# Clustered attention and two feed-forward blocks on one core: weight loads from ScalarE's queue, output transposes later in SyncE's queue, and 35 instead of 62 feed-forward steps issued during the heads

## The chip, the cores and the metric

One core of one Trainium2 chip. The metric is the device time of one execution in microseconds (us). The kernel before took 812.64 us as the median of 3 runs (808.35 to 814.8).

## The reference, cut to what matters

Shapes: 2 batches, 8 heads, 768 positions, head size 64, 16 clusters; then 1536 tokens of width 512, hidden width 2048.

```
q_assign = argmax(q_n @ c_n.T); k_assign = argmax(k_n @ c_n.T)      # cluster of each q and k
scores   = where(q_assign == k_assign, (q @ k.T) / 8, -1e9)
attn     = exp(scores - max) / (sum + 1e-9);  o = attn @ v          # 16 heads in all
x = o as (1536, 512)
x = softplus(x @ w_in1) @ w_out1
x = leaky_relu(x @ w_in2) @ w_out2      # leak 0.01
```

## The kernel before, in words

**Precision.** Matmuls run on f16 pairs: a value is held as a high and a low part, and a product is three matmuls (high by high, high by low, low by high).

**Order of the work.** The program gives every instruction a priority number, lower being more urgent (`at_pri`). A planner fixes each engine's order before the run: on its own model of time it gives an engine the most urgent instruction that is ready. On the chip each engine then takes its queue strictly in that order. A DMA stands in the queue of the engine that issues it, and if it must wait, all behind it in that queue wait too.

**Heads.** Each of the 16 heads goes through: loads of q and k (L173, L174) and v (L180); split and first transpose (`split`, `t<-n`, L197); cluster scores on TensorE (`as`, L206) and the one-hot rows on VectorE; two transposes (`tq<-nq` L232, `tk<-nk` L233); a first pass of scores for the row maximum (TensorE L244, VectorE L251); a third transpose (`tm<-nq`, L259); scores again (L277, L278), exponentials on ScalarE (L284), the product with v (L300 to L318) and the normalisation (L347 to L353). Work on a head starts two heads ahead. After each odd head two transposes (`xth<-xnh`, `xtl<-xnl`, L359) put two heads' output into the feed-forward's input. They stand at priority h+1-4, with head h's own work around h. All DMAs, these included, stand in SyncE's queue (SP).

**Feed-forward.** A stretch of 384 tokens (two per batch) goes through 16 tiles of `layer_in` (12 matmuls each, L414) and 16 steps of `layer_mid` (12 matmuls each, L427); the second block has `layer_in` and `layer_out` (L446). A tile of `layer_in` goes from PSUM through its activation into `g_h` and `g_l`. For batch 0 that is `act_ln_exp`: VectorE L392, ScalarE exp L393, ScalarE ln L394, VectorE L395, ScalarE L396, GpSimd L397, where L395 is the last to read the PSUM tile. For batch 1 it is `act_softplus`: ScalarE L382 and L383 read PSUM, VectorE L384 forms the low part. Exp and ln stand in one table of ScalarE; softplus needs an ACT_TABLE_LOAD. From head 8 on, steps of batch 0 are issued between the heads: `FF_RATE` of them for each of 47 slots, so 62 of 64. Step n has priority 8 + n/4. A step issued there takes its PSUM from a ring of two banks (`pm`). One issued behind the last head takes it from a pool of six (`pm2`), which holds the banks that the heads give back.

**Weights.** Each of four weight matrices comes in 16 pieces of 512 KB (`w_piece`): a load into one of two `st` buffers (L134), three VectorE operations that turn 64-bit floats into 32-bit ones (L142, L145, L148; the last one frees `st`), the high part on ScalarE (L152) and the low part on VectorE (L153). The first 32 pieces come during the heads; the second 32 have their place only when the heads' SBUF is given back.

Of the kernel before, what the change touches and what calls it, by code (L numbers as in the profile page):

```python
# [37 lines left out]
AHEAD = 2  # L38
LEAD_SPLIT, LEAD_ASSIGN, LEAD_MAX, LEAD_M, LEAD_LOAD, LEAD_NORM = 2.5, 2, 4, 2.5, 2, 4

FF_PRI, FF_STEP, FF_RATE = 8, 0.25, 1.333

W_FREE, W_FROM, W_TO, W_PER = 4, 8, 10, 5
W_PRI = ((0, 0.5), (17, 0.3))
# [7 lines left out]
def attn_moe_kernel(  # L52
# [12 lines left out]
    nc = tc.nc  # L65
    V, S, G, PE = nc.vector, nc.scalar, nc.gpsimd, nc.tensor
    B, H, SEQ, D = q.shape
    NCL = cen.shape[1]
    DM, DFF = w_in1.shape
    C = SEQ // 128  # L70
# [21 lines left out]
    def atile(shape, dt, tag, h):  # L92
        late, early = BUFS[tag]
        n = turn[tag] = turn.get(tag, -1) + 1
        if h < H and early and n % (late + early) >= late:
            return ep.tile(shape, dt, tag=tag, name=tag, bufs=early)
        return at.tile(shape, dt, tag=tag, name=tag, bufs=late)

    w_inh = const.tile([128, KDM, DFF], F16, name="w_inh")
    w_inl = const.tile([128, KDM, DFF], F16, name="w_inl")  # L100
    w_outh = const.tile([128, KFF, DM], F16, name="w_outh")
    w_outl = const.tile([128, KFF, DM], F16, name="w_outl")
    xt_h = [const.tile([128, KDM, SEQ], F16, name=f"xth{b}") for b in range(B)]
    xt_l = [const.tile([128, KDM, SEQ], F16, name=f"xtl{b}") for b in range(B)]
# [26 lines left out]

    def w_piece(dsth, dstl, src):
        st = wst.tile([128, 512, 2], I32, tag="st", name="st")
        nc.sync.dma_start(out=st, in_=src.rearrange("p (n t) -> p n t", t=2))  # L134

        def conv(bank=False):
            lo, hi = st[:, :, 0], st[:, :, 1]
            if bank:
                c = pm.tile([128, 512], I32, tag="m0", name="wcp")
            else:  # L140
                c = wst.tile([128, 512], I32, tag="wc", name="wc")
            V.tensor_scalar(  # L142
                out=c, in0=hi, scalar1=3, scalar2=0x3FFFFFFF, op0=ALU.logical_shift_left, op1=ALU.bitwise_and
            )
            V.scalar_tensor_tensor(  # L145
                out=c, in0=hi, scalar=-0x40000000, in1=c, op0=ALU.bitwise_and, op1=ALU.bitwise_or
            )
            V.scalar_tensor_tensor(  # L148
                out=c, in0=lo, scalar=29, in1=c, op0=ALU.logical_shift_right, op1=ALU.bitwise_or
            )  # L150
            cf = c.bitcast(F32)
            S.activation(out=dsth, in_=cf, func=AF.Copy, scale=WS)  # L152
            V.scalar_tensor_tensor(out=dstl, in0=cf, scalar=WS, in1=dsth, op0=ALU.mult, op1=ALU.subtract)  # L153

        return conv
# [8 lines left out]
    def out_pieces(w, wh, wl):  # L164
        wi = w.bitcast(I32)
        for kk in range(KFF):
            yield wh[:, kk, :], wl[:, kk, :], wi[kk * 128:(kk + 1) * 128, :]
# [170 lines left out]
    def emit_norm(h):  # L338
        b, hh = divmod(h, H)
        if hh % 2 == 0:  # L340
            xn_t[h // 2] = [atile([128, C, 128], F16, f"xn{n}", h) for n in "hl"]
        xh, xl = xn_t[h // 2]
        xps = x_t.pop(h)
        xv = xps[:, 0:C * XW].rearrange("p (c d) -> p c d", d=XW)
        dp = xps[:, C * XW:C * XW + C].unsqueeze(2)
        dd = atile([128, C, 1], F32, "dd", h)
        V.tensor_scalar(out=dp, in0=xv[:, :, D:XW], scalar1=1e-9, scalar2=1.0 / XS, op0=ALU.add, op1=ALU.mult)  # L347
        V.reciprocal(out=dd, in_=dp)
        y = atile([128, C, D], F32, "y", h)
        V.tensor_tensor(out=y, in0=xv[:, :, 0:D], in1=dd.to_broadcast([128, C, D]), op=ALU.mult)  # L350
        cs = slice((hh % 2) * D, (hh % 2) * D + D)
        S.copy(out=xh[:, :, cs], in_=y)
        G.tensor_tensor(out=xl[:, :, cs], in0=y, in1=xh[:, :, cs], op=ALU.subtract)  # L353
        for d_ in (tp1, tp2, tpq):
            d_.pop(h)
        if hh % 2 == 1:
            xn_t.pop(h // 2)
            for src, dst in ((xh, xt_h[b]), (xl, xt_l[b])):
                nc.sync.dma_start_transpose(  # L359
                    out=dst[:, hh // 2, :].rearrange("p (c r) -> p c r", c=C), in_=src.rearrange("p c d -> p (c d)")  # L360
                )


    pmx = [pm]
# [9 lines left out]
    def mps_next():  # L374
        if pmx[0] is pm:
            turn["m"] = 1 - turn.get("m", 0)
            return pm.tile([128, 512], F32, tag=f"m{turn['m']}", name="m")
        return pmx[0].tile([128, 512], F32, tag="m", name="m")
# [23 lines left out]
    def layer_in(b, t0, act, wh, wl):  # L402
        xh, xl = xt_h[b], xt_l[b]
        ts = slice(t0, t0 + TB)
        for m in range(KFF):
            hp = mps_next()[:, 0:TB]
            ms = slice(m * 128, (m + 1) * 128)
            ops = []
            for kk in range(KDM):
                ops += [(wh[:, kk, ms], xh[:, kk, ts]), (wh[:, kk, ms], xl[:, kk, ts])]  # L410
            for kk in range(KDM):
                ops += [(wl[:, kk, ms], xh[:, kk, ts])]
            for i, (w_, x_) in enumerate(ops):
                PE.matmul(out=hp, lhsT=w_, rhs=x_, start=(i == 0), stop=(i == len(ops) - 1))  # L414
            act(m, hp)
            yield

    def layer_mid(b, t0):
        xh, xl = xt_h[b], xt_l[b]
        ts = slice(t0, t0 + TB)  # L420
        for m in range(KDM):
            yp = mps_next()[:, 0:TB]
            ms = slice(m * 128, (m + 1) * 128)
            n = 0
            for kk in range(KFF):
                for w_, g_ in ((w_outh, late["h"]), (w_outh, late["l"]), (w_outl, late["h"])):
                    PE.matmul(out=yp, lhsT=w_[:, kk, ms], rhs=g_[:, kk, :], start=(n == 0), stop=(n == 3 * KFF - 1))  # L427
                    n += 1
                if kk % 4 == 3:
                    if kk == KFF - 1:  # L430
                        S.activation(out=xh[:, m, ts], in_=yp, func=AF.Copy, scale=1.0 / WS)
                        V.scalar_tensor_tensor(
                            out=xl[:, m, ts], in0=yp, scalar=1.0 / WS, in1=xh[:, m, ts], op0=ALU.mult, op1=ALU.subtract
                        )
                    yield
# [19 lines left out]
    def pri(x):  # L455
        return int(100000 + 10000 * x)

    @contextmanager
    def at_pri(x):
        old = tc.cur_priority  # L460
        tc.cur_priority = pri(x)
        yield
        tc.cur_priority = old
# [8 lines left out]
    with at_pri(-9):  # L472
# [6 lines left out]
            out=ss[:, 1:2], in0=ss[:, 0:1], scalar1=ss[:, 2:3], scalar2=ss[:, 1:2], op0=ALU.mult, op1=ALU.add  # L479
# [35 lines left out]
    def w_step():  # L515
        w0, wr = W_PRI[cnt["w"] >= 34]
        with at_pri(w0 + wr * (cnt["w"] % 34)):
            if convs:
                n = cnt["w"] - 1
                g = -1 if n < W_FREE else int(W_FROM + (W_TO - W_FROM) * (n - W_FREE) / (32 - W_FREE))  # L520
                g = min(g, max(mark, default=-1), 15)
                bank = n < KDM * DFF // 512
                if g >= 0:
                    with tc.issue_after(mark[g].ins):
                        convs.pop(0)(bank)
                else:
                    convs.pop(0)(bank)
            if wq:
                convs.append(w_piece(*wq.pop(0)))
        cnt["w"] += 1  # L530
# [7 lines left out]
    def moe1():  # L538
        wq.extend(out_pieces(w_out1, w_outh, w_outl))
        for b in range(B):  # L540
            for t0 in range(0, SEQ, TB):
                for _ in layer_in(b, t0, act_softplus if b else act_ln_exp, w_inh, w_inl):
                    w_step()
                    yield
                while (b, t0) == (0, 0) and (wq or convs):
                    w_step()
                for _ in layer_mid(b, t0):
                    w_step()
                    yield

    def moe2():
        for b in range(B):
            for t0 in range(0, SEQ, TB):
# [5 lines left out]
                yield from layer_out(b, t0, w_out2h, w_out2l)  # L559

    ff = m_steps(moe1())

    def chain(h):
# [22 lines left out]
    st = {"credit": 0.0}  # L586
# [72 lines left out]
```

## Time and profile before

| | |
|---|---|
| median of 3 runs | 812.64 us |
| profiled execution, device time | 808.4 us |
| its span in the trace | 806.6 us |
| TensorE busy | 736.2 us (91%) |
| VectorE / ScalarE / GpSimd busy | 408.4 / 328.7 / 175.3 us |
| mean granted TensorE clock | 0.968 |

The trace is of one execution. PE is TensorE, DVE VectorE, ACT ScalarE, POOL GpSimd, SP SyncE's queue of DMAs. L134 is line 134 of the kernel. In a tile's name "out<-in" buffer numbers are left out.

### The profile page before, as it was taken

The numbers are of one execution on the slowest core, as the hardware profiler recorded it, in microseconds if no ns is written. First come the engines' busy times: TensorE is split into PE (matmuls) and PEld (weight loads), VectorE is DVE, ScalarE is ACT, GpSimd is POOL, SyncE is SP. The second block draws the span as 40 slices with busy tenths as digits, with TensorE's granted clock in tenths as the row PEclk, the third lists the DMA queues.
The fourth block names the chain that finished last, engine by engine and source line by source line (L and its number), as shares of the span: only waits on it lengthen the run. The fifth ranks groups of instructions, "written<-read, shape, count | busy, mean of one in ns | idle before, by whom it ended". The sixth has DMA issues, their size and how long they took to land.

```text
span 806.6 us, 13925 instructions
## 1 busy us (share of the span) xinstructions
PE 736.2 (91%) x5664; PEld 454.1 (56%) x5664; DVE 408.4 (51%) x835; ACT 328.7 (41%) x755; POOL 175.3 (22%) x168
## 2 busy tenths in 40 slices
PE   2489989899899888998689999999999999999998
PEld 1167756576657556775355656666645645644643
DVE  4886767778899977237988931301200200200210
ACT  5266655656566533354535512403402411411410
POOL 5156646534344423331310000000000000000000
PEclk9998978979989999999999999999999999999999
DMA  8977445745757465103445400000000000000000
GB/s 197 207 184 136 96 105 129 166 115 137 168 145 164 124 142 113 23 9 116 132 137 176 158 27 1 1 1 1 1 14 27 1 14 26 1 14 27 1 14 26
DMA packets 104880, 66.01 MB, mean 82 GB/s; under 512 B 90992, under 2 KB 95088, under 8 KB 104816
## 3 DMA queue, kind: packets, MB, share of 16 engines
q1 hardware_dynamic: 104816, 65.13, 33.0%
q8 instruction: 44, 0.72, 0.4%
q14 instruction: 20, 0.16, 0.1%
HBM read 43.02 MB, written 3.15 MB: 57 GB/s over the span
## 4 chain that ended last, share of the span: by engine, by line
PE 62%; DMA 16%; DVE 14%; ACT 4%; issue 2%; SPq 1%; POOL 1%; DVEq 0%; ACTq 0%; POOLq 0%
PE m L414 22%; PE m L446 15%; PE m L427 9%; DMA st<-in_moe_w_out_dram 3%; PE x L300 3%; DMA st<-in_moe_w_in_dram 3%; DMA tm<-nq 3%; DMA t<-n 3%; PE s L278 2%; DVE wc L148 2%; PE s L244 2%; DVE wc L145 2%; PE s L277 2%; DVE mm L251 2%; DVE wc L142 2%
## 5 line engine op out<-in xcount | busy, mean ns | idle before, releaser
L384 DVE TENSOR_TENSOR g_l<-mr,g_h 128x384 f16<-128x384 f32 x96 | 53.4, 557 | 205.4 <-ACT mr L383 205.4
L251 DVE TENSOR_REDUCE mm<-s 128x1 f32<-128x384 f32 x192 | 103.0, 551 | 39.0 <-PE s L244 37.5
L286 POOL TENSOR_TENSOR pl<-p 128x768 f16<-128x768 f32 x56 | 83.2, 1490 | 101.6 <-ACT p L284 100.1
L414 PE MATMUL m<-xth,w_inh 128*128 128x384 f16 x256 | 84.9, 333 | 11.9 <-DVE mr L395 11.9
L284 ACT ACTIVATE p<-s 128x384 f32<-128x384 f32 x144 | 67.4, 489 | 54.2 <-PE s L278 49.6
L427 PE MATMUL m<-g_h,w_outh 128*128 128x384 f16 x256 | 84.0, 329 | 1.6 <-DVE mr L395 1.6
L427 PE MATMUL m<-g_l,w_outh 128*128 128x384 f16 x256 | 84.2, 329 | 1.2 <-DVE g_l L384 1.1
L414 PE MATMUL m<-xtl,w_inh 128*128 128x384 f16 x256 | 84.8, 332 | 0.0
L427 PE MATMUL m<-g_h,w_outl 128*128 128x384 f16 x256 | 83.9, 328 | 0.5 <-DVE w_outl L153 0.4
L414 PE MATMUL m<-xth,w_in2h 128*128 128x384 f16 x256 | 83.3, 326 | 0.0
L414 PE MATMUL m<-xtl,w_in2h 128*128 128x384 f16 x256 | 83.3, 326 | 0.0
L382 ACT ACTIVATE g_h<-m 128x384 f16<-128x384 f32 x96 | 46.7, 491 | 86.4 <-PE m L414 86.4
L244 PE MATMUL s<-tk,tq 80*128 80x384 f16 x192 | 67.1, 365 | 15.1 <-DVE mm L251 9.2
L414 PEld LDWEIGHTS <-w_inh 128*128 128x128 f16 x512 | 50.5, 100 | 46.2 <-issue 16.5
L446 PE MATMUL m<-w_out2h,g_h 128*128 128x512 f16 x192 | 72.8, 379 | 0.0
L446 PE MATMUL m<-w_out2l,g_h 128*128 128x512 f16 x192 | 72.8, 379 | 0.0
L446 PE MATMUL m<-w_out2h,g_l 128*128 128x512 f16 x192 | 72.8, 379 | 0.0
L427 PEld LDWEIGHTS <-w_outh 128*128 128x128 f16 x512 | 50.2, 99 | 34.6 <-issue 3.2
L414 PEld LDWEIGHTS <-w_in2h 128*128 128x128 f16 x512 | 50.1, 98 | 33.4
L446 PEld LDWEIGHTS <-g_h 128*128 128x128 f16 x384 | 37.6, 98 | 44.9
L278 PE MATMUL s<-tm,tk 81*128 81x384 f16 x160 | 55.4, 359 | 8.1 <-DMA tm<-nq 7.9
L277 PE MATMUL s<-t 128*128 128x384 f16 x160 | 56.1, 352 | 4.6 <-ACT p L284 4.2
(108 smaller groups left out, 1303.2 us busy)
## 6 DMA issues: line engine op xcount, KB each, us to landing
st<-in_moe_w_in_dram SPq DMA_DIRECT2D x32, 512.0 KB, 4.1
st<-in_moe_w_out_dram SPq DMA_DIRECT2D x32, 512.0 KB, 3.6
qk<-in_q_dram SPq DMA_DIRECT2D x16, 192.0 KB, 3.2
qk<-in_k_dram SPq DMA_DIRECT2D x16, 192.0 KB, 3.1
v<-in_v_dram SPq DMA_DIRECT2D x16, 192.0 KB, 3.5
out_dram<-ob SPq DMA_DIRECT2D x12, 256.0 KB, 2.0
t<-n SPq DMA_TRANSPOSE x16, 4.0
tq<-nq SPq DMA_TRANSPOSE x16, 4.2
```

Of the source, the lines that this page charges most:

```text
L244: PE.matmul(out=o, lhsT=t[0:KS1, c, :], rhs=tk[0:KS1, 3 * j:3 * j + 3, :], start=True, stop=True,)
L251: V.reduce_max(out=mms[h % 2][:, c, j:j + 1], in_=bank[:, 0:3 * 128], axis=AX)
L277: PE.matmul(out=o, lhsT=t1[:, kt, 1, :], rhs=t1[:, 3 * j:3 * j + 3, 0, :], start=True, stop=False)
L278: PE.matmul(out=o, lhsT=t2[0:KS2, kt, :], rhs=tqh[0:KS2, 3 * j:3 * j + 3, :], start=False, stop=True)
L284: S.activation(out=p[:, j, :], in_=sp, func=AF.Exp, scale=scale)
L286: G.tensor_tensor(out=pl, in0=p, in1=pb, op=ALU.subtract)
L300: PE.matmul(out=xps[:, c * XW:(c + 1) * XW], lhsT=pf[:, c * 128:(c + 1) * 128], rhs=v32s[h % V_BUFS][:, kt, :], start=(kt == 0 and c == 0) ...
L382: S.activation(out=late["h"][:, m, :], in_=hp, func=func, scale=scale, alpha=alpha)
L384: V.tensor_tensor(out=late["l"][:, m, :], in0=r, in1=late["h"][:, m, :], op=ALU.subtract)
L414: PE.matmul(out=hp, lhsT=w_, rhs=x_, start=(i == 0), stop=(i == len(ops) - 1))
L427: PE.matmul(out=yp, lhsT=w_[:, kk, ms], rhs=g_[:, kk, :], start=(n == 0), stop=(n == 3 * KFF - 1))
L446: PE.matmul(out=op, lhsT=g_[:, kk, rs], rhs=w_[:, kk, :], start=(n == 0), stop=(n == 3 * KFF - 1))
```

## The change

Three edits. The weight loads (L134) are issued by ScalarE instead of SyncE. The two output transposes (L359) get priority h+1 instead of h+1-4, except for the last pair of each batch, which keeps its place. `FF_RATE` falls from 1.333 to 0.75, so that 35 of the 64 steps of batch 0 are issued during the heads and 29 behind them (before: 62 and 2). The second stretch of batch 0 takes `act_softplus` in place of `act_ln_exp`.

```
-FF_PRI, FF_STEP, FF_RATE = 8, 0.25, 1.333
+FF_PRI, FF_STEP, FF_RATE = 8, 0.25, 0.75
...
-        nc.sync.dma_start(out=st, in_=src.rearrange("p (n t) -> p n t", t=2))
+        S.dma_start(out=st, in_=src.rearrange("p (n t) -> p n t", t=2))
...
-            for src, dst in ((xh, xt_h[b]), (xl, xt_l[b])):
-                nc.sync.dma_start_transpose(
-                    out=dst[:, hh // 2, :].rearrange("p (c r) -> p c r", c=C), in_=src.rearrange("p c d -> p (c d)")
-                )
+            with at_pri(h + 1 if hh < H - 1 else h + 1 - LEAD_NORM):
+                for src, dst in ((xh, xt_h[b]), (xl, xt_l[b])):
+                    nc.sync.dma_start_transpose(
+                        out=dst[:, hh // 2, :].rearrange("p (c r) -> p c r", c=C), in_=src.rearrange("p c d -> p (c d)")
+                    )
...
-                for _ in layer_in(b, t0, act_softplus if b else act_ln_exp, w_inh, w_inl):
+                for _ in layer_in(b, t0, act_softplus if b or t0 else act_ln_exp, w_inh, w_inl):
```

## Rows read from the trace of the kernel before

**Rows 1.** The page: the span, and TensorE's busy tenths in 40 equal slices.
```profile
span 806.6 us, 13925 instructions
...
PE   2489989899899888998689999999999999999998
```
**Rows 2.** One window: start:end, length, busy us (instructions) by engine, clock, DMA.
```profile
380.00:400.00 20.00, 11.29 (x65) 6.16 (x64) 18.17 (x31) 10.68 (x21) 5.35 (x5) 1.00 0.43 136
```
**Rows 3.** The chain that ended last: start us, us, what.
```profile
23.57 8.48 DMA t<-n
...
153.31 5.62 DMA t<-n
...
345.27 1.95 PE m L414 x12
...
467.51 23.89 PE m L427 x146
491.40 31.20 PE m L414 x192
```
**Rows 4.** Waits from 345 to 420 us: who waited for whom, total us, times, longest.
```profile
PE m L414 <- DVE mr L395: 10.7, 7, 2.5
...
PE m L427 <- DVE mr L395: 1.6, 1, 1.6
```
**Rows 5.** Groups by line: names, shapes, count | busy us, mean ns | idle before, releasers.
```profile
L427 PE MATMUL m<-g_l,w_outh 128*128 128x384 f16 x256 | 84.2, 329 | 1.2 <-DVE g_l L384 1.1
...
L277 PE MATMUL s<-t 128*128 128x384 f16 x160 | 56.1, 352 | 4.6 <-ACT p L284 4.2 <-DVE pl L282 0.2
...
L384 DVE TENSOR_TENSOR g_l<-mr,g_h 128x384 f16<-128x384 f32 x96 | 53.4, 557 | 205.4 <-ACT mr L383 205.4
...
L382 ACT ACTIVATE g_h<-m 128x384 f16<-128x384 f32 x96 | 46.7, 491 | 86.4 <-PE m L414 86.4
...
L382 ACT ACT_TABLE_LOAD x2 | 2.6, 1283 | 0.0
```
**Rows 6.** Timelines of TensorE, ScalarE and VectorE around the last head's end.
```profile
361.08 0.33 PE L414 MATMUL m<-xth,w_inh 128*128 128x384 f16 x1
...
354.34 0.87 ACT L284 ACTIVATE p<-s 128x384 f32<-128x384 f32 x2 [0.30 <-PE s L278]
...
359.88 0.55 DVE L350 TENSOR_TENSOR y<-x,dd 128x384 f32<-128x384 f32 x1
```
**Rows 7.** ScalarE's timeline at the first softplus.
```profile
436.82 1.28 ACT L382 ACT_TABLE_LOAD   x1
438.11 0.49 ACT L382 ACTIVATE g_h<-m 128x384 f16<-128x384 f32 x1
```
**Rows 8.** Waits of SyncE's queue from 0 to 345 us, columns as in rows 4.
```profile
SPq L134 <- DVE wc L148: 34.6, 11, 9.0
...
SPq L134 <- DVE wcp L148: 11.4, 5, 5.2
```
**Rows 9.** Timeline of SyncE's queue, at two places: start us, us, engine, line.
```profile
22.82 0.64 SPq L134 DMA_DIRECT2D st<-in_moe_w_in_dram  x1
...
133.46 1.22 SPq L359 DMA_TRANSPOSE xth<-xnh  x1
...
137.92 1.46 SPq L233 DMA_TRANSPOSE tk<-nk  x1
```
**Rows 10.** TensorE's timeline where it waited for two of these transposes.
```profile
141.41 0.49 PE L244 MATMUL s<-tk,tq 80*128 80x384 f16 x2 [1.18 <-DMA tk<-nk]
...
158.97 0.38 PE L206 MATMUL as<-ct,t 128*128 128x16 f16 x9 [2.63 <-DMA t<-n]
```
**Rows 11.** The heads' 300 us and one early window, columns as in rows 2.
```profile
40.00:340.00 300.00, 273.51 (x2899) 195.42 (x2899) 233.18 (x486) 166.89 (x405) 139.51 (x117) 0.91 0.57 131
...
4.00:8.00 4.00, 0.00 (x0) 0.00 (x0) 3.83 (x14) 3.36 (x9) 3.54 (x4) 1.00 0.96 265
```
**Rows 12.** The page's DMA issues: out<-in, KB each, median us to landing.
```profile
t<-n SPq DMA_TRANSPOSE x16, 4.0
```

## The prediction

> **What bounds it now.** I read the slices first, then windows, then the chain of waits, then who waited. In the slices TensorE (PE) is nearly full except in the first two slices and around the twentieth [rows 1]. The window of that one, 380 to 400 us, has PE busy for 11.29 of 20 us and VectorE for 18.17 [rows 2]. The chain ends in whole stages of PE without a gap: from 467.51 us on nothing stands between the stages, and 16 tiles of layer_in take 31.20 us, 1.95 us a tile [rows 3]. So the end is set by PE's work plus PE's idle time ahead of 467 us, and the question for each edit is which idle it removes or adds.
>
> The largest idle after the heads is one kind: PE waits for L395, the last operation of the exp-and-ln softplus that frees a PSUM tile: 10.7 us in 7 waits and 1.6 us once more [rows 4]. One further gap, 1.1 us, is a wait for L384 [rows 5]. Together 13.4 us. The reader is to see why: an exp-and-ln tile crosses engines four times before its PSUM is free, two of them on VectorE, and VectorE is at that time full of weight conversions [rows 2].
>
> **Edit 1, the activation of the second stretch and the later steps.** Although 62 steps are issued during the heads, the second stretch's first tile runs at 345.27 us, when the heads are nearly over [rows 3]. Sixteen tiles change from exp-and-ln to softplus. PSUM is then free after two ScalarE passes of about 491 ns, with one VectorE operation of 557 ns behind them that PE does not wait for directly [rows 5]. The same softplus beside the same conversions ran later in this trace, and its only PE wait was the 1.1 us one [rows 5]. So I remove all 13.4 us and put 2.2 back, for two such stretches instead of one. Bounds on what stays: 0, and 6 us if ScalarE, which now also issues the loads, falls behind on half of the tiles.
>
> The price is the pool. Steps beyond 35 take their banks from the heads, so they wait for the last head's normalisation, which read its bank until 360.43 us (359.88 + 0.55). In the run before, two tiles of this kind had been worked by 361.08, when the next one starts [rows 6]. Now they come after 360.43: two tiles are 3.9 us, less the 0.65 us between 360.43 and 361.08, so **+3.3 us**.
>
> The three tiles that keep the old ring run beside the last head's exponentials (the last at 354.34 [rows 6]), and softplus needs a table switch of 1.28 us [rows 5, 7]. Each return to exp needs another. On the last head's path I count one switch there and one back, 2.6 us, against one tile of 1.95 us that no longer stands between that head's matmuls: **+0.6 us**. Bounds: -2 us (no switch before the last exp) and +5.7 us (three there, three back, 7.7 - 1.95). In this trace the next activation starts at 438.11, right where the load ends [rows 7]. The Trainium skill (ScalarE: Activation LUTs, What ACT_TABLE_LOAD costs) gives the same 1283 ns but adds a drain, about 2.66 us in all for each switch; the trace shows no drain behind the load, and with it the two switches would cost 2.7 us more and the sum end at -7.0.
>
> **Edit 2, weight loads on ScalarE.** For SyncE it removes 64 issues, one of which took 0.64 us [rows 9], and 46.0 us of waiting for L148 in 16 waits during the heads [rows 8]. What stood behind these was mostly not due yet, so I do not credit them as such. One place counts: loads share a queue with transposes, and the t<-n transpose at 153.31 took 5.62 us and PE waited 2.63 us for it; the median is 4.0 [rows 3, 10, 12]. I credit that 1.6 us.
>
> For ScalarE it adds 32 issues during the heads. At 0.45 us (between nothing, if issue hides behind a running activation, and 0.64) they are 14.4 us; ScalarE is busy 166.89 of 300 us there, so they fit [rows 11]. PE's waits for exponentials were 4.2 us [rows 5]; scaled by 14.4/166.89 that is **+0.4 us**. The waits are the greater risk. L152 of the same piece already stands in ScalarE's queue waiting for L148, and the load two pieces on becomes ready at the same moment, so I take no added wait; the upper bound is the 46.0 us. Queued behind a blocked load would be the exponentials (L284), with PE waiting, and the splits of the head two ahead. The other 32 loads come after the heads. From 467.51 on 86 us of the first block (23.89 + 31.20 and a layer_mid of the same 31.20) still stand ahead of the first matmul that needs these weights [rows 3]; that covers them, and what they could hold up is softplus, which is in the 6 us above.
>
> At the start SyncE's queue is full of more urgent work, and the second load comes at 22.82 us [rows 9]. On ScalarE, idle while q and k land, they can go at 2 us. That costs the first heads bandwidth (DMA share is 0.96 at 4 to 8 us, 265 GB/s [rows 11]) and spares the t<-n that took 8.48 us against 4.0 [rows 3, 12]. Ends: +8 us (four more loads ahead of 32 us, 2.1 MB at 265 GB/s) and -4.5 us. I take 0, since the same bytes move either way.
>
> **Edit 3, output transposes later.** Each of six pairs stands further back in SyncE's queue; the two that close a batch stay. At 133.46 the queue stood until head 5's output was there, and loads, tq and tk went out behind it, tk at 137.92; PE then waited 1.18 us for that tk [rows 9, 10]. **-1.2 us**. Bounds: 0, and -8 us if each of the three pairs of batch 0 cost as much and more. Their outputs are not read before the stretch begins, so lateness costs nothing while two buffers hold.
>
> **The sum.** -13.4 + 2.2 + 3.3 + 0.6 - 1.6 + 0.4 - 1.2 = -9.7 us against the profiled execution's 808.4: 798.7. That execution lies 4.2 us under the median of 812.64, so on the scale of the medians **802.9 us**.
>
> **Rivals.**
> - *A: ScalarE stands still behind loads (slower).* The planner places a load where its model says that L148 is done; on the chip VectorE lags, which is what SyncE's waits for it show [rows 8]. If half of the 46.0 us falls on exponentials that PE needs, the sum is -9.7 - 0.4 + 23 = +12.9: 825.5. It decides once more than about 10 of the 46 us reach PE. Against it: ScalarE has 133 us of slack in the heads [rows 11].
> - *B: the start is bound by DMA, and another queue gives no bandwidth.* Loads move ahead of the heads' own data; half of the +8 us stays, and the transposes gain nothing (+1.6): -9.7 + 4 + 1.6 = -4.1: 808.5. For it: the 0.96 share. Against: what comes early is gone later. The Trainium skill (DMA: Bandwidth & Descriptors, Issuing engines are not separate DMA queues) says that DMAs from any engine run on the same 16 DMA engines and interleave; the share in the early window agrees with a shared limit, and the page speaks for this rival.
> - *C: exp and softplus alternate in the last head.* Six switches, +5.7 instead of +0.6, and the pool opens that much later: -4.6: 808.
> - *D: SyncE's relief is large.* -8 instead of -1.2 for edit 3: -16.5: 796.
> - *E: the planner's order hardly changes what SyncE does, and softplus queues behind loads.* Edits 2 and 3 give nothing and 6 us of idle stay: -9.7 + 2.8 + 3.8 = -3.1: 809.5.
>
> **How the numbers follow.** Forecast 0.42, A 0.15, B 0.16, C 0.10, D 0.07, E 0.10. The time is the forecast's. From no change a measurement of this kernel can tell about 1%, 8.1 us: under 804.5 is faster, over 820.8 slower. The forecast lies 1.6 us inside faster, so of its 0.42 I give 0.37 to faster and 0.05 to the same; D is faster; of the 0.36 of B, C and E, 0.30 lie within, 0.03 in faster and 0.03 in slower (B's whole +8 us with part of A's waits); A is slower for 0.13 and within for 0.02. Faster 0.47, same 0.37, slower 0.16. The range runs from 793 (D with no idle left) to 820; the forecast's own is 798 to 808.
>
> **What would show it.** Right: no PE wait for L395 after the heads and a layer_in of 1.95 us a tile once the banks are free; mid steps about 10 us earlier than 467.51 for the last gap; one or two more ACT_TABLE_LOADs than two at L382; a tk without a wait behind L359. Wrong: weight loads in ScalarE's timeline with idle time ahead of exponentials; the first cluster scores or the first tm later than before; L350 of the last head well after 359.88; or PE idle between the last head's products and the first pm2 tile by more than 3 us.

## The result and the profile after

The changed kernel took 823.49 us as the median of 4 runs (821.12 to 828.97), the kernel before 813.29 us beside it (808.35 to 814.8): a ratio of 1.0119, interval 1.0072 to 1.0166. It is slower, where 802.9 us was forecast, and above the range's 820. Run again beside other kernels it took 819.02 us (10 runs), ratio 1.0057 [1.0018, 1.0095]: slower again, though inside the range. The ratios, here and below, use only executions in the faster of the chip's two states and are not the quotients of the medians. The profiled execution of the changed kernel, 828.97 us with a span of 827.1, is the slowest of the first four, and that of the kernel before, 808.4 us, stands at the lower end of its own. So the two traces differ by 20.5 us where the medians differ by 10.2.

The page after, where [rows 1] stood: span, busy time of TensorE, its busy tenths and its clock in 40 slices.
```profile
span 827.1 us, 13824 instructions
...
PE 749.8 (91%) x5664; PEld 459.9 (56%) x5664; DVE 394.8 (48%) x819; ACT 324.7 (39%) x743; POOL 161.7 (20%) x152
...
PE   0398988788988899998998989999999999999998
...
PEclk9998888679998998997999999999999999999999
```
The hole in the twentieth slice is gone, as forecast. The first two slices fell from 2 and 4 to 0 and 3. PE has as many matmuls as before (5664) but is busy for 13.6 us more (736.2 before): it ran more of them at a lower clock. The other 6.9 of the 20.5 us are idle time.

Two windows, columns as in [rows 2, 11]: the one of the old hole, and the heads.
```profile
380.00:400.00 20.00, 18.84 (x104) 10.76 (x104) 9.93 (x20) 8.87 (x18) 0.91 (x1) 0.83 0.27 73
...
40.00:340.00 300.00, 267.23 (x2711) 185.69 (x2710) 227.95 (x481) 161.00 (x389) 135.03 (x113) 0.87 0.58 126
```
From 380 to 400 us PE is busy 18.84 us instead of 11.29, but at a clock of 0.83. In the heads the clock fell from 0.91 to 0.87. ScalarE, which now issues the loads, is no fuller than before, 161.00 us against 166.89; the issuing of a DMA is not counted in this.

The groups that answer to [rows 4, 5], columns as there.
```profile
L415 PE MATMUL m<-xth,w_inh 128*128 128x384 f16 x256 | 87.3, 342 | 5.4 <-DVE xtl L433 2.1 <-DVE mr L396 1.3 <-DVE y L350 1.2
...
L428 PE MATMUL m<-g_l,w_outh 128*128 128x384 f16 x256 | 84.6, 331 | 3.4 <-DVE g_l L385 3.4
...
L385 DVE TENSOR_TENSOR g_l<-mr,g_h 128x384 f16<-128x384 f32 x112 | 62.4, 557 | 220.6 <-ACT mr L384 220.6
```
Lines are one higher than before from L360 on. PE's waits for the exp-and-ln tile (L395, now L396) are down from the 12.3 us of [rows 4] to 1.3, and g_l rose from 1.1 to 3.4: of the 13.4 us forecast to go, 8.7 went. PE's idle time behind the last head fell from 13.5 to 6.9 us, by 6.6, where the terms of edit 1 that stand there (-13.4 + 2.2 + 3.3) gave 7.9. So the tail did about what it should. The rest of the trace is where it was lost.

The start. Row maxima of the first two heads (L256), columns: operation, min/median/max ns, first and last start us. After, a second profile of the same changed kernel (e9_after below), then before.
```profile
L256 DVE TENSOR_REDUCE nq<-mm x2: 173/178/184, 43.1 to 55.5; 128x6 f16<-128x18 f32 x2
```
```profile
L256 DVE TENSOR_REDUCE nq<-mm x2: 174/178/183, 38.8 to 50.5; 128x6 f16<-128x18 f32 x2
```
```profile
L256 DVE TENSOR_REDUCE nq<-mm x2: 177/178/178, 35.1 to 51.0; 128x6 f16<-128x18 f32 x2
```
The first head is 8.0 us later in the first profile and 3.7 in the second, and in the second the next head has already made it up (50.5 against 51.0). Up to 40 us PE had done 8.71 and 12.12 us of work, against 13.21 before: 4.5 and 1.1 us less. Why the first head is late, is in three timelines of the changed kernel: ScalarE's queue, SyncE's queue, TensorE.
```profile
0.77 0.87 ACTq L134 DMA_DIRECT2D st<-in_moe_w_in_dram  x2
...
7.50 0.33 ACTq L134 DMA_DIRECT2D st<-in_moe_w_in_dram  x1
...
13.49 0.34 ACTq L134 DMA_DIRECT2D st<-in_moe_w_in_dram  x1
...
17.46 0.33 ACTq L134 DMA_DIRECT2D st<-in_moe_w_in_dram  x1
...
21.77 0.33 ACTq L134 DMA_DIRECT2D st<-in_moe_w_in_dram  x1
```
```profile
15.76 3.90 SPq L197 DMA_TRANSPOSE t<-n  x1
```
```profile
28.52 0.81 PE L206 MATMUL as<-ct,t 128*128 128x16 f16 x24 [7.19 <-DMA t<-n]
```
Six loads are out by 22 us, where the second one stood at 22.82 before [rows 9]. The t<-n transpose issued at 15.76 landed at 28.48, with the loads of 13.49 and 17.46 among what was in flight beside it, and PE waited 7.19 us for it. The chain and the page, where [rows 3, 12] stood, show the same later on:
```profile
32.52 5.33 DMA t<-n
...
486.66 25.20 PE m L428 x146
511.86 31.20 PE m L415 x192
```
```profile
t<-n SPq DMA_TRANSPOSE x16, 5.4
```
The median t<-n takes 5.4 us, against 4.0. The last gap ends at 486.66, against 467.51 before.

ScalarE's timeline around the last head, where [rows 6, 7] stood:
```profile
365.81 1.28 ACT L383 ACT_TABLE_LOAD   x1
367.11 0.49 ACT L383 ACTIVATE g_h<-m 128x384 f16<-128x384 f32 x1
...
369.06 1.28 ACT L284 ACT_TABLE_LOAD   x1
...
371.24 1.28 ACT L383 ACT_TABLE_LOAD   x1
...
373.43 1.28 ACT L284 ACT_TABLE_LOAD   x1
...
386.08 1.28 ACT L383 ACT_TABLE_LOAD   x1 [3.61 <-PE m L415]
```
Five table loads stand where none stood. The activation follows its load within 20 ns (365.81 + 1.28, then 367.11).

### The profile page after: what moved, and what is told of

The parts are those of the page before. It is cut to its first block, busy times and chain, and to the rows that moved or that the text cites. A ratio compares the mean times of both kernels' runs of the same rounds, so it can differ in the third digit from the quotient of the medians.

```text
span 827.1 us, 13824 instructions
## 1 busy us (share of the span) xinstructions
PE 749.8 (91%) x5664; PEld 459.9 (56%) x5664; DVE 394.8 (48%) x819; ACT 324.7 (39%) x743; POOL 161.7 (20%) x152
## 3 DMA queue, kind: packets, MB, share of 16 engines
q10 hardware_dynamic: 9216, 33.56, 13.7%
## 4 chain that ended last, share of the span: by engine, by line
PE 63%; DMA 18%; DVE 14%; ACT 2%; issue 2%; SPq 0%; POOL 0%; ACTq 0%; DVEq 0%; POOLq 0%
PE m L415 23%; PE m L447 15%; PE m L428 9%; DMA st<-in_moe_w_in_dram 4%; DMA st<-in_moe_w_out_dram 4%; DMA t<-n 3%; PE x L300 3%; DMA tm<-nq 3%; PE s L278 3%; PE s L244 3%; DVE wc L145 2%; DVE wc L148 2%; DVE mm L251 2%; DMA tk<-nk 2%; PE s L277 2%
## 5 line engine op out<-in xcount | busy, mean ns | idle before, releaser
L385 DVE TENSOR_TENSOR g_l<-mr,g_h 128x384 f16<-128x384 f32 x112 | 62.4, 557 | 220.6 <-ACT mr L384 220.6
L415 PE MATMUL m<-xth,w_inh 128*128 128x384 f16 x256 | 87.3, 342 | 5.4 <-DVE xtl L433 2.1
L383 ACT ACTIVATE g_h<-m 128x384 f16<-128x384 f32 x112 | 54.6, 487 | 87.4 <-PE m L415 87.3
L415 PE MATMUL m<-xtl,w_inh 128*128 128x384 f16 x256 | 87.1, 341 | 0.3 <-DMA xtl<-xnl 0.3
L244 PE MATMUL s<-tk,tq 80*128 80x384 f16 x192 | 69.0, 380 | 13.4 <-DVE mm L251 8.3
L415 PEld LDWEIGHTS <-w_inh 128*128 128x128 f16 x512 | 51.8, 102 | 41.3 <-issue 10.9
L278 PE MATMUL s<-tm,tk 81*128 81x384 f16 x160 | 57.8, 374 | 10.9 <-DMA tm<-nq 10.9
```

The costliest lines, as they stand in the source:

```text
L244: PE.matmul(out=o, lhsT=t[0:KS1, c, :], rhs=tk[0:KS1, 3 * j:3 * j + 3, :], start=True, stop=True,)
L278: PE.matmul(out=o, lhsT=t2[0:KS2, kt, :], rhs=tqh[0:KS2, 3 * j:3 * j + 3, :], start=False, stop=True)
L383: S.activation(out=late["h"][:, m, :], in_=hp, func=func, scale=scale, alpha=alpha)
L385: V.tensor_tensor(out=late["l"][:, m, :], in0=r, in1=late["h"][:, m, :], op=ALU.subtract)
```

## The experiments

Each kernel was timed beside the kernel before on the same chip, in three rounds. Edit 1 is the feed-forward edit, edit 2 the loads, edit 3 the output transposes. "First row max" is the start of L256 of head 0; "last head" is the start of its last L350, whose end is 0.55 us later; both are of one profiled execution.

| kernel | median us | ratio to before, 95% | first row max / last head / span |
|---|---|---|---|
| before | 812 to 816 | 1 | 35.1 / 359.9 / 806.6 |
| after | 823.49 | 1.0119 [1.0072, 1.0166] | 43.1 / 381.4 / 827.1 |
| e9_after (the same again) | 819.02 | 1.0057 [1.0018, 1.0095] | 38.8 / 365.6 / 810.6 |
| e1_loads (edit 2 alone) | 819.27 | 1.0062 [1.0029, 1.0095] | 39.1 / 378.2 / 820.9 |
| e2_ff (edit 1 alone) | 813.09 | 1.0008 [0.997, 1.0046] | 34.1 / 363.6 / 807.4 |
| e3_tr (edit 3 alone) | 807.43 | 0.9919 [0.9883, 0.9955] | 33.6 / 358.2 / 809.0 |
| e4_ff_tr (edits 1 and 3) | 807.13 | 0.9947 [0.9909, 0.9985] | 33.9 / 356.4 / 801.5 |
| e5_first6 | 812.42 | 0.9990 [0.9958, 1.0022] | 34.4 / 367.9 / 810.5 |
| e7_first6act | 811.75 | 0.9993 [0.9961, 1.0026] | 41.3 / 370.0 / 814.9 |
| e6_w2act | 812.82 | 1.0006 [0.9967, 1.0044] | 33.9 / 363.1 / 805.9 |
| e8_mix | 803.84 | 0.9896 [0.984, 0.9952] | 33.8 / 355.6 / 802.2 |
| e10_hold | 823.83 | 1.0162 [1.0097, 1.0228] | 36.9 / 377.9 / 822.0 |
| e11_sliver | 812.24 | 0.9987 [0.9958, 1.0017] | 34.9 / 357.8 / 808.3 |
| e12_mix85 | 801.76 | 0.9878 [0.9832, 0.9924] | 34.3 / 363.1 / 803.1 |
| e13_lite | 803.92 | 0.9778 [0.9681, 0.9874] | 34.5 / 365.9 / 803.6 |
| e14_litesp | 787.18 | 0.9639 [0.9582, 0.9695] | 33.1 / 348.4 / 785.9 |
| e15_replan_sp | 812.80 | 1.0013 [0.997, 1.0056] | 34.1 / 364.4 / 811.5 |
| e16_replan_act | 812.86 | 1.0029 [0.9983, 1.0075] | 38.3 / 367.4 / 810.6 |
| e17_replan2_sp | 814.01 | 1.0021 [0.998, 1.0063] | 37.2 / 360.8 / 805.8 |
| e18_replan2_act | 816.26 | 1.0061 [1.0018, 1.0105] | 39.1 / 371.6 / 815.0 |

### One edit at a time

The diffs are those of the change, each applied alone to the kernel before; the fourth has edits 1 and 3.

e1_loads, only edit 2: 

> Only the weight loads go to ScalarE; the rest is the kernel before. Theory S (the loads cost the time: six go out within 22 us and take DMA bandwidth from the first heads, later ones run beside the transposes and slow them): +12 to +18 us over before, first row maximum (L256) at about 43 us instead of 35, t<-n over 5 us in the median. Theory F (the feed-forward edit costs the time: table switches and the wait for the banks at the last head): within 3 us of before. Theory T (the later output transposes hold up SyncE's queue): within 3 us of before.

e2_ff, only edit 1: 

> Only the feed-forward edit: FF_RATE 0.75 and softplus for the second stretch; loads and output transposes as before. Theory S: 4 to 9 us faster than before, since the 13.4 us of waits for the old activation go and only some come back as table switches. Theory F: 5 us or more slower than before, with at least four table loads at the last head. Theory T: as theory S. First row maximum at 35 us in all of them.

e3_tr, only edit 3: 

> Only the later output transposes. Theory S and theory F: within 3 us of before. Theory T: 5 us or more slower, with heads 6 to 8 late by that much while the first row maximum stays at 35 us.

e4_ff_tr, edits 1 and 3: 

> The changed kernel with all weight loads back on SyncE. Theory S: 12 to 20 us faster than the changed kernel, so 803 to 812, first row maximum at 35 us. Theory F: still 5 us or more over before. Theory T: still 5 us or more over before, lost between heads 5 and 8.

Edit 2 alone makes the kernel slower, edit 1 alone changes nothing that can be measured, edit 3 alone is faster. With the loads back on SyncE the other two edits gave 0.9947. Theory S held for e4_ff_tr (803 to 812), but missed the size of each single edit: 12 to 18 us for edit 2 was 5 by the ratio (6.9 by the medians), 4 to 9 us gained by edit 1 was nothing, and edit 3, expected within 3 us, was 6.6 faster. Nor do the single effects add up: by the ratios they are +5.0, +0.7 and -6.6 us, -0.9 together, and the kernel with all three is 4.6 and 9.7 us slower than the kernel before. The first row maximum is at 34 us in each kernel with loads on SyncE and at 39 to 43 us with them on ScalarE.

Why edit 1 gives nothing: the table loads of e2_ff, and windows from 345 to 370 us (length, PE busy, clock, DMA share, GB/s) of e2_ff, then of before.
```profile
L382 ACT ACT_TABLE_LOAD x5 | 6.4, 1283 | 3.7 <-PE m L414 3.6
...
L284 ACT ACT_TABLE_LOAD x3 | 3.8, 1283 | 0.1
```
```profile
345.00:370.00 25.00, 21.01 (x181) 0.87 0.09 17
```
```profile
345.00:370.00 25.00, 25.00 (x201) 1.00 0.09 17
```
Seven of these loads stand between 348 and 369 us, on both sides of the last head's exponentials. PE, full before, is idle for 4.0 of 25 us there and the clock falls to 0.87. PE's idle time after the last head did fall, from 13.5 to 5.9 us. That head ended 3.7 us later and PE's busy time rose by 7.3 us (736.2 to 743.5), so the span gained nothing (806.6 and 807.4). Up to 350 us e2_ff has TensorE's order of before. So the planner's order in the heads plays no part here; and the lower clock from 40 to 160 us (0.86 against 0.89), which makes up part of the 7.3 us, is a difference between two executions of the same order.

### Which loads cost the time

e5_first6, the first six loads on SyncE and the rest on ScalarE; e7_first6act, the reverse; e6_w2act, the first 32 on SyncE:
```
-        S.dma_start(out=st, in_=src.rearrange("p (n t) -> p n t", t=2))
+        turn["w"] = turn.get("w", -1) + 1
+        (nc.sync if turn["w"] < 6 else S).dma_start(out=st, in_=src.rearrange("p (n t) -> p n t", t=2))
```


> The changed kernel with the first six weight loads back on SyncE, the other 58 on ScalarE. Theory S-start (edit 2 costs through the six loads in the first 22 us alone): all of the 14 us by which the changed kernel and the one with all loads on SyncE differ comes back, 807 to 811, first row maximum at 34 to 35 us. Theory S-middle (it costs in heads 5 to 8, where loads on a queue of their own slow the heads' transfers): 815 to 820, first row maximum at 35 us but row maximum 8 still 10 us late against 156. Half each: about 814.

> The complement: the first six loads on ScalarE, the other 58 on SyncE, edits 1 and 3 as changed. Theory S-start: 819 to 824, as the changed kernel, first row maximum at 40 to 43 us. Theory S-middle: 807 to 812, the late start made up by head 3 (in the run with edit 2 alone row maximum 3 was on time again). Half each: about 815.

> The changed kernel with the first 32 loads (those during the heads) on SyncE and the second 32 on ScalarE. Both theories of edit 2 put its cost into the heads: 805 to 810, the same as with all loads on SyncE (807). If ScalarE is held up behind the late loads (my prediction's rival A, after the heads): 812 or more, with PE idle over 10 us after the last head.

With the first six back on SyncE the start is restored (34.4), with only these on ScalarE it is not (e7_first6act, a line lower):
```profile
L257 DVE TENSOR_REDUCE nq<-mm x1: 171/171/171, 41.3 to 41.3; 128x6 f16<-128x18 f32 x1
```
So the early loads are what moves the start. But all three totals lie within 0.2% of before and 0.4 to 0.6% above e4_ff_tr, also where the early loads are on SyncE. The total isn't explained by the start alone: the total of e7_first6act, late at the start, came out where the theory of a start made up later put it (807 to 812). The parts do not add up either. e9_after, the changed kernel again, was expected at 813 to 816 if the two partial moves' costs added, and took 819.02. The 812.82 us of e6_w2act fit the total of rival A's theory, but PE's idle time after the last head is 4.4 us there and not over 10: the late loads did not hold up ScalarE.

e10_hold keeps all loads on ScalarE and ties the first six behind work of head 0 to 2:
```
+        n = turn["w"] = turn.get("w", -1) + 1
+        if n < 6:
+            with tc.issue_after(held[("el", "m", "m")[n // 2], max(0, n // 2 - 1)].ins):
+                S.dma_start(out=st, in_=src.rearrange("p (n t) -> p n t", t=2))
```


> All loads stay on ScalarE, but the first six are queued behind head work there: two behind head 0's one-hot rows (about 15 us), two behind its row maximum (about 36 us), two behind head 1's. If the early cost is the bytes that go ahead of the heads' own loads: first row maximum back at 34 to 37 us and 4 to 8 us faster than the changed kernel beside it. If it is the second queue as such: first row maximum at 39 us or later and no gain.

It did not recover; it is the slowest of all. The first row maximum came back (36.9) and then the second head lost more. Two queues, ScalarE, VectorE and TensorE of e10_hold:
```profile
37.11 0.35 ACTq L138 DMA_DIRECT2D st<-in_moe_w_in_dram  x1
37.50 0.54 ACTq L138 DMA_DIRECT2D st<-in_moe_w_in_dram  x1
38.08 2.13 SPq L265 DMA_TRANSPOSE tm<-nq  x1
...
46.95 0.69 DVE L148 TENSOR_SCALAR wcp<-st 128x512 int32<-128x512 int32 x1 [6.16 <-DMA st<-in_moe_w_in_dram]
...
48.97 0.51 ACT L199 CAST nq<-qk 128x384 f16<-128x384 f32 x1 [11.55 <-DMA tm<-nq]
```
```profile
48.41 0.48 PE L250 MATMUL s<-tk,tq 80*128 80x384 f16 x1 [7.10 <-DVE mm L257]
```
With two loads and the heads' own transfers in flight beside it, the tm<-nq issued at 38.08 landed at 48.89, after 10.8 us (the median of its kind is 2.9 in before), and a conversion at the head of VectorE's queue waited 6.16 us for the late load, with the row maxima that PE needed behind it. So it isn't how early the loads are, but what they land beside and what waits for them.

e11_sliver lets ScalarE issue 16 of the 512 columns of each piece and SyncE the rest:
```
-        nc.sync.dma_start(out=st, in_=src.rearrange("p (n t) -> p n t", t=2))
+        sr = src.rearrange("p (n t) -> p n t", t=2)
+        S.dma_start(out=st[:, 0:16], in_=sr[:, 0:16])
+        nc.sync.dma_start(out=st[:, 16:512], in_=sr[:, 16:512])
```


> Edits 1 and 3 with every load split: ScalarE issues the first 16 of 512 columns of each piece, SyncE the other 496. ScalarE's queue so carries the 64 issues and waits of the change and 3 percent of its bytes. If ScalarE's issue time or its waits in order cost the time (my rival A): 815 to 825, near the changed kernel. If the bytes on a queue of their own do: 805 to 811, as with all loads on SyncE, and PE's waits for DMA between heads 7 and 15 at 2 to 5 us instead of 8 to 12.

0.9987, with a start of 34.9 and a last head at 357.8, both near e4_ff_tr (33.9, 356.4). PE's waits for DMA from 40 us to the last head's end are 11.6 us, against 13.7 there. ScalarE's issuing as such did not hold up the heads; what its total lost against e4_ff_tr stands in the tail (450.5 us from the last head to the end, against 445.1), where no cause was found.

### Bytes, queue, or the luck of the order

e13_lite and e14_litesp, loads on ScalarE and on SyncE:
```
-        st = wst.tile([128, 512, 2], I32, tag="st", name="st")
+        st = wst.tile([128, 64, 2], I32, tag="st", name="st")
...
-            lo, hi = st[:, :, 0], st[:, :, 1]
+            lo, hi = (st[:, None, :, j].to_broadcast([128, 8, 64]) for j in (0, 1))
```


> The changed kernel with every weight load still issued by ScalarE, but each load brings 64 of the 512 columns (an eighth of the bytes), and the conversions read these eight times over, so their instructions and sizes stay. Left out: seven eighths of the weights. Theory 'bytes beside the heads' transfers': the loads' own issue costs nothing, so the ratio to before falls from 1.006 to 1.012 to about 0.99, the same within 0.5% as the next kernel (the same small loads on SyncE); first row max back to 34 or 35 us, and the transposes of t under 4.8 us on average. Rival 'issue and order': ScalarE's issuing and the order that the planner makes of it cost the time; then it stays at 1.005 or above and 1% or more above the next kernel.

> Edits 1 and 3 with the loads left on SyncE, each load bringing an eighth of the bytes as in the kernel beside it. Left out: seven eighths of the weights. Theory 'bytes beside the heads' transfers': 0.987 to 0.995, at or a little under the 0.995 that the same kernel had with whole loads, since on one queue loads and transposes mostly went one after the other anyway. Rival 'issue and order': the same here; the two kernels are told apart by their distance, 0 against 1% or more.

The first row maximum came back on ScalarE's queue too (34.5), so the early loads' bytes are what delayed it. But both kernels gained 3% by losing the bytes (0.9947 to 0.9639, and 1.0057 or 1.0119 to 0.9778), and they stayed 1.4% apart. The two intervals just touch; the single executions do not (795.65 to 808.23 us, and 786.21 to 790.28). The transposes no longer differ: t<-n took 4.0 and 4.1 us on the mean. The theory that bytes alone make the difference fell. The pages (span, busy) and the heads' windows of e13_lite, then e14_litesp:
```profile
span 803.6 us, 13843 instructions
...
40.00:340.00 300.00, 273.53 (x2845) 196.41 (x2845) 227.43 (x475) 166.38 (x398) 139.22 (x116) 0.88 0.39 78
```
```profile
span 785.9 us, 13883 instructions
...
40.00:340.00 300.00, 278.50 (x3032) 200.06 (x3031) 232.49 (x486) 177.15 (x418) 144.33 (x120) 0.94 0.40 78
```
DMA moves the same in both (78 GB/s), yet one has a clock of 0.88 in the heads and the other 0.94. PE's busy time differs by 11.8 us (742.2 and 730.4), its idle time by 5.9: two thirds of the distance is PE's busy time, the same matmuls at a lower clock. Moving a load also makes the planner write another order for every engine, so the last four kernels changed the order alone, by one number of the planner: LEAD_ASSIGN 2 to 2.2 in e15_replan_sp (on SyncE) and e16_replan_act (on ScalarE), LEAD_LOAD 2 to 1.8 in e17_replan2_sp, LEAD_ASSIGN 2 to 1.7 in e18_replan2_act.
```
-LEAD_SPLIT, LEAD_ASSIGN, LEAD_MAX, LEAD_M, LEAD_LOAD, LEAD_NORM = 2.5, 2, 4, 2.5, 2, 4
+LEAD_SPLIT, LEAD_ASSIGN, LEAD_MAX, LEAD_M, LEAD_LOAD, LEAD_NORM = 2.5, 2.2, 4, 2.5, 2, 4
```


> Edits 1 and 3, loads on SyncE, with one number of the planner changed (LEAD_ASSIGN 2 to 2.2), so that it makes another order from head 8 on and nothing else differs. Theory 'the queue': loads on SyncE cost less whatever the order, so 0.990 to 0.999, below its counterpart on ScalarE by 0.8% or more. Rival 'the luck of the order': any new order costs about 0.5 to 1%, so 1.000 to 1.005, and no clear distance from the counterpart.

> The changed kernel with the same number changed (LEAD_ASSIGN 2 to 2.2). 'The queue': 1.004 to 1.014, as the changed kernel itself. 'The luck of the order': anywhere from 0.993 to 1.010, and within 0.5% of its counterpart on SyncE.

> Edits 1 and 3, loads on SyncE, with LEAD_LOAD 1.8 instead of 2, which gives another order from the second head on. 'The queue': 0.990 to 1.000. 'The luck of the order': 1.000 to 1.008.

> The changed kernel with LEAD_ASSIGN 1.7 instead of 2, another order from head 6 on. 'The queue': 1.004 to 1.014. 'The luck of the order': 0.993 to 1.010, within 0.5% of the kernel before it.

Neither theory held whole. With edits 1 and 3 and loads on SyncE, three orders gave 0.9947, 1.0013 and 1.0021, mean 0.9994; with loads on ScalarE three orders gave 1.0088 (the mean of the two measurements of after), 1.0029 and 1.0061, mean 1.0059. The means are 0.65% or 5.3 us apart, but the two sides nearly touch: e15_replan_sp and e16_replan_act cannot be told apart. So a new order alone moves this kernel by some 0.4% either way, e4_ff_tr was one of the lucky ones, and the queue costs about 5 us more. From the totals alone that is not sure: 0.65% is little over twice the standard error of 0.29% that this scatter leaves on the difference of two means of three.

The traces tell the two sides apart. PE's longest waits for DMA from 40 us to the last head's end: in e9_after, then in e4_ff_tr (who waited for whom, total us, times, longest).
```profile
PE s L278 <- DMA tm<-nq: 9.9, 8, 2.6
PE s L244 <- DMA tk<-nk: 7.2, 4, 3.0
...
PE as L206 <- DMA t<-n: 3.7, 5, 1.2
```
```profile
PE s L278 <- DMA tm<-nq: 8.5, 7, 3.1
...
PE as L206 <- DMA t<-n: 4.3, 4, 1.7
...
PE s L244 <- DMA tk<-nk: 0.9, 1, 0.9
```
Such waits add up to 20.1 to 22.8 us in the four profiles with all three edits (after twice, e16, e18) and to 13.4 to 16.0 in the three with the loads on SyncE (e4, e15, e17). All of PE's waits there are 33.1 to 36.9 us and 27.4 to 31.3, about 5 us apart on the means. With edit 2 alone the waits for DMA are 24.5 us against 17.1 in before. With the first six loads on ScalarE they are 17.2 (e7_first6act), with only the later ones 25.2 (e5_first6), and with all on ScalarE but an eighth of the bytes 15.2 (e13_lite). So the later loads make these waits, and by their bytes. The waits are not the whole total: e5_first6 has the most of them and ends at 0.9990.

The start is the smaller part. In six profiles with the early loads on ScalarE and free to go (after twice, e1, e7, e16, e18) the first row maximum stands at 38.3 to 43.1, mean 40.0; in those with the early loads on SyncE, e17_replan2_sp with 37.2 aside, at 33.1 to 35.1. But in four of the six the second head's stands at 50.5 to 51.4, as in before (51.0), and PE had done 11.78 to 12.54 us of work by 40 us, 0.7 to 1.4 less than before; only after's first profile (55.5; 8.71) and e7_first6act (53.5; 9.81) lost more.

### The versions that the experiments point to

e8_mix: edits 1 and 3, loads on SyncE, and the first three tiles of the second stretch keep exp-and-ln, so that no softplus stands between the last head's exponentials. e12_mix85: the same with five such tiles and FF_RATE 0.85.
```
+    def act_late(m, hp):
+        (act_ln_exp if m < 3 else act_softplus)(m, hp)
...
-                for _ in layer_in(b, t0, act_softplus if b or t0 else act_ln_exp, w_inh, w_inl):
+                for _ in layer_in(b, t0, act_softplus if b else (act_late if t0 else act_ln_exp), w_inh, w_inl):
```


> Edits 1 and 3 with all loads on SyncE, but the second stretch's first three tiles, those that run beside the last head, keep exp-and-ln; the other 13 take softplus. If the table switches at the last head cost what their row says: seven loads become one there, the last head ends 3 to 6 us earlier relative to its row maximum, and the time is 801 to 804. If ScalarE's time there is hidden: 805 to 809, as with softplus for all.

> A candidate: edits 1 and 3, loads on SyncE, FF_RATE 0.85 (39 steps issued in the heads, so that seven tiles of the second stretch may use the old ring beside the last head), exp-and-ln for the first five of them and softplus for the other eleven. If the wait for the heads' banks costs what I worked out for two tiles (3.3 us): 2 to 4 us faster than the version with three such tiles (803.8), so 800 to 802. If that wait is hidden: 803 to 806.

e8_mix has TensorE's and SyncE's order of e4_ff_tr and only other activations beside the last head: 803.84 against 807.13 us. The intervals overlap, but the traces say what went: from the last head's row maximum to its end e8_mix needs 29.5 us, e4_ff_tr 34.6. Windows from 345 to 370 us, e4_ff_tr, then e12_mix85, and the only table load of e12_mix85 near the last head:
```profile
345.00:370.00 25.00, 20.00 (x141) 0.86 0.11 19
```
```profile
345.00:370.00 25.00, 25.00 (x226) 1.00 0.09 17
...
365.52 1.28 ACT L383 ACT_TABLE_LOAD   x1
```
PE is full through the last head at full clock, and e12_mix85, 0.9878, beats both kernels. As its heads have an order of their own, part of its 1.2% may be order, and its 2.1 us under e8_mix are too few to show what the wait for the heads' banks costs.

## Why the prediction was wrong

Two steps failed, at about the same weight: the price of edit 2 and the tables of edit 1. Edit 2 was taken at -1.2 us (-1.6 for the transposes, +0.4 for the issues, 0 for the early start) and measured +5.0 alone. Of the early start it says: "Ends: +8 us ... and -4.5 us. I take 0, since the same bytes move either way." The first row maximum came 8.0 us later in the profile of after, 3.7 in its second one and 4.9 on the mean of the six profiles (40.0 less 35.1), and by 40 us PE had done 4.5 and 1.1 us less work. The -1.6 us for the transposes had the wrong sign: PE's waits for DMA in the heads rose from 17.1 us to 22.8 and 20.8. The bytes are the same, the order in which they land is not: on SyncE a load stood behind the transposes that the first heads need; on a queue of its own it goes beside them. The Trainium skill (DMA: Bandwidth & Descriptors, Issuing engines are not separate DMA queues) says that such DMAs interleave on the same 16 engines and that a second issuer saves only sequencer time; the trace agrees on the interleaving, and shows in addition that the interleaving costs whoever was urgent: a t<-n with a load in flight took 6.9 us on the mean in after and 4.8 in before, and 4.6 and 4.2 without one. With a load in flight it took 5.3 to 6.2 us in e9, e1, e16 and e18, where ScalarE issues the loads, and 5.0 in e4, e15 and e17, where SyncE does.

- **Rival B** (the start bound by DMA, the transposes gain nothing) was the right mechanism. Half of the +8 us is near the 4.9 by which the first row maximum moved; the transposes did not only gain nothing, they lost. Its 808.5 came with edit 1's full gain.
- **Edit 1** was to give 7.3 us and gave none (e2_ff, 1.0008 [0.997, 1.0046]). The L395 waits went nearly as forecast, and the pool opened in time: PE stood 1.16 us between the last head's work and the first pool tile. The term that failed is the tables: +0.6 was taken, with a bound of +5.7; **rival C** with six switches is what happened, five in the profile of after and seven in e2_ff. In e2_ff's window from 345 to 370 us PE lost 4.0 us of idle time and, as an estimate from its clock (0.13 of 25 us), 3.3 us of work: together the 7.3 us that edit 1 was to give. The mean of the three orders with edits 1 and 3 is 0.9994.
- **Rival A** (ScalarE stands behind loads) did not happen: PE's waits for exponentials were 2.8 us in after and 4.2 in before [rows 5], and e11_sliver, with all issues on ScalarE, kept its heads on time. The direction that it warned of came by another way.
- **Edit 3** measured 0.9919 alone, some 6.6 us, toward its bound of -8 (**rival D**). PE's waits for DMA in the heads were 12.3 us, against 17.1 in before and 15.1 in e2_ff, whose SyncE and TensorE order is that of before up to 350 us. As an order alone is worth about 0.4% here, how much of the gain is the moved transposes stays open.
- **What no term held** is the clock. All terms were sums of idle time; in the two traces, the slowest execution after against one of the fastest before, 13.6 of 20.5 us are the same matmuls at a lower clock.

What stays open: why the three edits together cost 5.5 to 10.6 us more than the sum of the single ones, where an order is worth some 3.3 us and the 95% intervals of the four ratios together allow about 6; why one order's clock in the heads is better than another's; and e11_sliver's tail.

## What to carry to other kernels

A bulk load moved to an idle engine's queue is no longer held back by the urgent transfers ahead of it; before moving it, list which small transfers it will land beside and who waits for them, and price that from the rows where the two already overlapped. When an activation is exchanged to free PSUM sooner, read the timeline for the other table's users between the first and the last exchanged tile, and change over in one place. Before half a per cent is put down to an edit, change a planner's number that should not matter: the scatter of such orders is the bound on what one timing can show.

## What the runs showed of the hardware

**A wait of TensorE can cost twice.** TensorE of the kernel after at the last head's end:
```profile
375.26 0.32 PE L277 MATMUL s<-t 128*128 128x384 f16 x1 [1.84 <-ACT p L284]
...
377.26 0.51 PE L318 MATMUL x<-v,pl 128*128 128x65 f16 x6 [0.81 <-POOL pl L286]
...
380.31 0.51 PE L336 MATMUL x<-svr,tm 2*128 2x65 f16 x6
381.98 0.50 PE L415 MATMUL m<-xth,w_inh 128*128 128x384 f16 x1 [1.16 <-DVE y L350]
382.27 0.53 PE L415 MATMUL m<-xtl,w_inh 128*128 128x384 f16 x1
```
From 367 to 376 us the granted clock is 1.00; behind the idle times of 1.84 and 0.81 us it is 0.50, the 1.2 GHz level, from 377 to 387 us, and the matmul that took 0.33 us in [rows 6] takes 0.53. Not each wait does this: in before PE is busy for only 11.29 us from 380 to 400, and the clock stays at 1.00 [rows 2]. What makes the difference is not shown here. From run to run the time goes with the clock: over the 31 executions of the kernel before that stand beside the last four kernels (803.34 to 817.32 us), the clock goes from 0.952 to 0.970 with a correlation of -0.72 to the time, 6.6 us for each 0.01; which of the two moves the other, this does not say.

**Loads cost their bytes on either queue.** Seven eighths of the weight bytes less gave, by the ratios to the kernel before, 25 us on SyncE (0.9947 to 0.9639) and 23 to 28 on ScalarE, though hardly any instruction of TensorE names a load as what it waited for.

**A transpose issued beside a load of another queue can hold its own queue longer.** The t<-n of 15.76 kept SyncE's queue for 3.90 us; in e4_ff_tr the one of 12.74, with q and k in flight but no weight load, kept it for 1.92. Over the 16 of each kernel, those with a load in flight took 2.30 us to issue in after and the others 1.66; in before, with the loads in the same queue, 1.74 and 1.66.
